# Batch 1's norms and turns moved one batch earlier, squares of batches 1 and 2 on GpSimd, dense work moved later

## The chip, the cores and the metric

One core of a Trainium2 chip. The metric is the time of one execution in microseconds (us), as the device measures it; several executions are taken of each kernel. PE is TensorE, PEld its weight loads, DVE VectorE, ACT ScalarE, POOL GpSimd. The span of a trace is 1.8 to 2.5 us shorter than the time of the same run. Each run is marked by its state; one run of experiment 5 and one of the kernel before beside it are marked slow and left out of the ratios, the single runs of experiments 13 to 15 are of unknown state, and all others are marked fast.

## The reference, cut to what matters

```python
q_n = q / (norm(q) + 1e-6);  k_n = k / (norm(k) + 1e-6)      # 8 batches, 12 heads, 448 x 64
attn = softmax(q_n @ k_n.T / tau)
x = (attn @ v), heads side by side                            # 3584 x 768
out = leaky_relu(x @ w_in) @ w_out                            # 768 -> 2048 -> 768
```

## The kernel before

Each batch has twelve visits (pair of heads p, half): scores of one half pair, then row sums and value products that are owed from an earlier group, then the norm work of the next batch, then dense work (the two-layer network on rows that are ready) until a budget is met, then turns. A turn is a transpose on TensorE of a pair's normalised q and k with copies by DVE. The dense work is a list that is worked off in order; the budget (in us, as the kernel's author estimated them) only sets how far each visit goes. Its first layer gives tiles, each followed by a Prelu (the leaky ReLU) on ACT; its second layer gives blocks of 16 matmuls.

```python
inp = ctx.enter_context(tc.tile_pool(name="inp", bufs=1))     # q_n and k_n: one buffer each
ppv = ... bufs=2   # row sums and value products (PSUM)
pmm = ... bufs=2   # dense tiles, second-layer blocks and turned pairs (PSUM)
...
def norm_squares(b, what, eng, ...):  eng.tensor_mul(sq, x, x)       # written into q_n / k_n
def norm_reduce(b, what, ...):        nc.vector.tensor_reduce(...)
def norm_root(b, what, ...):          nc.scalar Ln, then Exp(0.5 x)
def norm_inverse(b, what, ...):       nc.vector: + 1e-6, reciprocal
def norm_apply(b, what, eng, ...):    eng.tensor_tensor(x * 1/norm)  # 2 instructions a group
...
        if b == 1:                    # cut: visits 0 to 5 hold the norms of batch 1's groups 1 and 2
            elif n == 6:
                norm_sums(2, "q")     # squares and sums on DVE
            elif n == 7:
                norm_sums(2, "k")
            elif n == 8:
                norm_root(2, "q"); norm_inverse(2, "q"); norm_apply(2, "q", P)
            elif n == 9:
                norm_root(2, "k"); norm_inverse(2, "k")
                norm_apply(2, "k", V, 0, 1)
                norm_apply(2, "k", P, 1, 3)
    turns = {(0, 9): (1, 0), (0, 10): (1, 1), (1, 3): (1, 2), (1, 4): (1, 3), (1, 5): (1, 4, 5),
             (1, 10): (2, 0, 1), (1, 11): (2, 2, 3), (2, 1): (2, 4, 5)}
```

Two facts carry the argument. The squares are written into the tile that the normalised values will fill, and that tile has one buffer. And DVE, ACT and GpSimd each work off their own list in order, so an instruction waits for the one written before it even if it needs nothing from it: in the changed kernel's trace DVE starts to copy a pair at 101.47 us that TensorE had turned by 96.6, because six multiplies stand before it.

## Time and profile before

| | before |
|---|---|
| time | 478.54 us, median of 3 (477.88 to 478.78) |
| span of the traced run | 477.8 us (its time was 480.28 us; it is not among the three) |
| TensorE busy | 435.0 us, 91% |
| TensorE idle from 39.4 to 116.8 us | 13.6 us |
| of it behind DVE's reciprocals | 6.7 us |

TensorE is the bound and its idle time in batch 1's visits is the target. The prediction below shows the lines and how they are read.

### The profile page before, as it was taken

To read this page: it belongs to the slowest core of one execution; us is meant where nothing else is said; L and a number is where in the kernel's file an instruction comes from. 1 tells how busy PE (TensorE), PEld (TensorE's weight loads), DVE (VectorE), ACT (ScalarE), POOL (GpSimd) and SP (SyncE) were. 2 spreads that over 40 slices of the span, in tenths; PEclk is the share of its full clock that TensorE was granted. 3 is DMA by queue.
4 is the path that set the end of the run, shared out by engine and by line. 5 is a ranking of instruction groups with operands and counts; after the bars stand their busy time and mean duration, and the time that the engine had idled before them with its cause. 6 is when DMAs were issued, how large, how long until landed. Compare 5 with 4: busy or idle time off the path is not lost.

```text
span 477.8 us, 8541 instructions
## 1 busy us (share of the span) xinstructions
PE 435.0 (91%) x3632; PEld 221.9 (46%) x3632; DVE 219.4 (46%) x269; ACT 269.7 (56%) x445; POOL 126.6 (27%) x150
## 2 busy tenths in 40 slices
PE   0788976779899999989899999998999999999996
PEld 0465633444344554444344554444434554454463
DVE  5964677967913186206823186218711311321000
ACT  3765665736764557654674557664765567533411
POOL 6552308065083012800083013700180000000000
PEclk9999999979999999998999999999999999999999
DMA  9999991808629660393329560455034110020022
GB/s 118 211 200 203 187 168 34 115 1 122 85 45 135 137 109 2 66 213 56 56 48 135 133 108 1 59 125 92 0 59 92 58 42 1 18 66 18 0 67 66
DMA packets 73924, 41.23 MB, mean 86 GB/s; under 512 B 29600, under 2 KB 73120, under 8 KB 73888
## 3 DMA queue, kind: packets, MB, share of 16 engines
q0 software_dynamic: 37728, 22.81, 34.6%
q1 hardware_dynamic: 36160, 17.90, 16.2%
q8 instruction: 28, 0.46, 0.4%
q14 instruction: 8, 0.07, 0.0%
HBM read 45.61 MB, written 11.01 MB: 119 GB/s over the span
## 4 chain that ended last, share of the span: by engine, by line
PE 76%; DMA 9%; DVE 6%; issue 4%; ACT 3%; POOL 1%; SPq 0%; POOLq 0%; ACTq 0%
PE mm L319 29%; PE mm L306 28%; PE pv L239 11%; PE sc L206 7%; DMA w_in_sb<-in_moe_w_in_dram 5%; DVE rs L262 2%; DMA kT<-k_n 2%; ACT pe L234 2%; DMA qk_bf<-in_q_dram 2%; DVE k_ni L127 1%; DVE k_n L124 1%; DVE q_n L124 1%; ACT hT L311 1%; PE sc L224 1%; PE mm L180 1%
## 5 line engine op out<-in xcount | busy, mean ns | idle before, releaser
L234 ACT ACTIVATE pe<-sc 112x896 bf16<-112x896 f32 (+2 forms) x192 | 168.1, 917 | 15.3 <-PE sc L224 8.1
L306 PE MATMUL mm<-xT,w_in_sb 128*128 128x512 bf16 (+3 forms) x864 | 157.3, 335 | 1.3 <-ACT hT L311 0.9
L319 PE MATMUL mm<-w_out_sb,hT 128*128 128x384 bf16 x896 | 154.0, 327 | 0.0
L262 DVE RECIPROCAL rs<-pv 128x448 f32<-128x448 f32 (+2 forms) x27 | 71.4, 2644 | 157.2 <-PE pv L239 157.1
L319 PEld LDWEIGHTS <-hT 128*128 128x128 bf16 x896 | 84.9, 98 | 67.0 <-issue 13.6
L306 PEld LDWEIGHTS <-w_in_sb 128*128 128x128 bf16 x864 | 77.9, 99 | 76.6 <-issue 17.4
L311 ACT ACTIVATE hT<-mm 128x512 bf16<-128x512 f32 (+3 forms) x144 | 71.9, 502 | 69.4 <-PE mm L306 69.0
L325 ACT COPY osb<-mm 128x384 f32<-128x384 f32 x56 | 26.8, 478 | 104.6 <-PE mm L319 74.0
L152 POOL TENSOR_TENSOR q_n<-qk_bf,q_ni 112x512 bf16<-112x512 bf16 x40 | 41.3, 1061 | 103.5 <-DVE q_ni L145 64.4
L206 PE MATMUL sc<-qT,kT 64*128 64x448 bf16 (+1 forms) x336 | 50.2, 362 | 10.2 <-ACT pe L234 7.2
L239 PE MATMUL pv<-pe,v_bf 112*32 112x448 bf16 (+2 forms) x864 | 48.9, 349 | 9.6 <-DVE rs L262 9.5
L152 POOL TENSOR_TENSOR k_n<-qk_bf,k_ni 112x512 bf16<-112x512 bf16 x44 | 46.6, 1085 | 15.8 <-DVE k_ni L145 15.8
L239 PEld LDWEIGHTS <-v_bf 112*32 112x32 bf16 x864 | 21.6, 100 | 29.7 <-issue 19.1
L92 POOL DMA_DIRECT2D v_bf<-in_v_dram x8 | 7.6, 944 | 101.0 <-PE pv L239 101.0
L206 PEld LDWEIGHTS <-kT 64*128 64x128 bf16 (+1 forms) x336 | 13.2, 103 | 40.2 <-issue 36.0
L127 DVE TENSOR_REDUCE k_ni<-k_n 112x16 f32<-112x1024 bf16 (+1 forms) x12 | 27.4, 2284 | 0.3
L127 DVE TENSOR_REDUCE q_ni<-q_n 112x16 f32<-112x1024 bf16 (+1 forms) x12 | 27.4, 2284 | 0.3
L239 PE MATMUL pv<-pe,ones 112*32 112x448 bf16 (+2 forms) x432 | 24.8, 346 | 1.0 <-ACT pe L234 1.0
L281 DVE TENSOR_TENSOR xT<-pv,rs 128x384 bf16<-128x384 f32 (+2 forms) x30 | 14.3, 477 | 22.9 <-PE pv L239 21.4
L278 DVE TENSOR_TENSOR xT<-pv,rs 128x448 bf16<-128x448 f32 x24 | 15.0, 625 | 19.7 <-PE pv L239 18.4
L180 PE MATMUL mm<-ident,q_n 112*128 112x112 bf16 x72 | 7.8, 241 | 10.9 <-DVE q_n L152 10.7
L124 DVE TENSOR_TENSOR q_n<-qk_bf 112x1024 bf16<-112x1024 bf16 x21 | 14.1, 719 | 4.7 <-DMA qk_bf<-in_q_dram 4.7
(48 smaller groups left out, 154.9 us busy)
## 6 DMA issues: line engine op xcount, KB each, us to landing
v_bf<-in_v_dram POOLq DMA_DIRECT2D x8, 672.0 KB, 7.5
qk_bf<-in_q_dram POOLq DMA_DIRECT2D x6, 672.0 KB, 7.4
qk_bf<-in_k_dram POOLq DMA_DIRECT2D x6, 672.0 KB, 10.8
w_in_sb<-in_moe_w_in_dram POOLq DMA_DIRECT2D x4, 768.0 KB, 19.9
w_out_sb<-in_moe_w_out_dram POOLq DMA_DIRECT2D x2, 1536.0 KB, 27.5
out_dram<-osb SPq DMA_DIRECT2D x16, 168.0 KB, 2.4
out_dram<-osb SPq DMA_DIRECT2D x16, 144.0 KB, 2.1
out_dram<-osb SPq DMA_DIRECT2D x16, 120.0 KB, 2.0
```

Of the source, the lines that this page charges most:

```text
L124: eng.tensor_mul(sq, x, x)
L127: nc.vector.tensor_reduce(st[what + "i", b][:, g0:g1].rearrange("p g a t -> p (g a) t"), squares(b, what, g0, g1).rearrange("p g a t d -> ...
L152: eng.tensor_tensor(out=xn[:, g, j].rearrange("p t h d -> p h t d"), in0=x[:, g, 2 * j : 2 * j + 2], in1=ni_j.unsqueeze(3).to_broadcast([P ...
L206: nc.tensor.matmul(out=sc[:wide, a, :S], lhsT=kT[r, o : o + wide], rhs=qT[r, p * S : (p + 1) * S], start=True, stop=True,)
L234: nc.scalar.activation(out=pe, in_=sc, func=ACTF.Exp, scale=inv_tau)
L239: nc.tensor.matmul(out=dst[32 * a : 32 * a + 32, c0:c1], lhsT=weights(a, ki), rhs=st["pe", b, 2 * g + a // 2][:, ki, a % 2, c0:c1], start= ...
L262: nc.vector.reciprocal(st["rs", b, g][:, c0:c1], sm[:, c0:c1])
L278: nc.vector.tensor_mul(x[:, kt, 64:512], po, rs)
L306: nc.tensor.matmul(out=pm[:, :n], lhsT=w_in_sb[:, kt, m * 128 : (m + 1) * 128], rhs=st["x", b][:, kt, x0 : x0 + n], start=(kt == 0), stop= ...
L311: nc.scalar.activation(out=st["h", c][:, m, :n], in_=pm[:, :n], func=ACTF.Prelu, alpha=0.01)
L319: nc.tensor.matmul(out=po[:, :NH], lhsT=st["h", c][:, m, j0 : j0 + 128], rhs=w_out_sb[:, m, n * NH : (n + 1) * NH], start=(m == 0), stop=( ...
L325: nc.scalar.copy(out=osb, in_=po[:, :NH])
```

## The change

Its intent is to give TensorE less to wait for in batch 1's visits: batch 1's norms go where DVE and GpSimd were idle, DVE loses the squares, and some dense work goes from batch 0 into batch 1's visits to cover the waits there. Cut to its core:

```diff
+        if b == 0:
+            if n == 0:   both(1, 0, 1, "squares", P, P)
+            ...          # cut: sums, roots and multiplies of groups 0 and 1 up to visit 9
+            elif n == 11: both(1, 2, 3, "reduce")
+        elif n == 1:     both(1, 2, 3, "root"); load(2, "v")
+        elif n == 2:     both(1, 2, 3, "apply", V, P)
         elif n == 4:
+            step(2, "q", 0, 3, ("squares", P)); load(3, "q")
+        elif n == 5:
+            step(2, "k", 0, 3, ("squares", P)); load(3, "k")
         elif n == 6:
+            step(2, "q", 0, 3, ("reduce", V))
         elif n == 7:
+            step(2, "k", 0, 3, ("reduce", V)); step(2, "q", 0, 3, ("root", A))
+        elif n == 8:
+            step(2, "q", 0, 3, ("apply", P)); step(2, "k", 0, 3, ("root", A))
+        elif n == 9:
+            step(2, "k", 0, 3, ("apply", V))
-                norm_apply(2, "k", V, 0, 1)
-                norm_apply(2, "k", P, 1, 3)
     turns = {
-        (0, 9): (1, 0), (0, 10): (1, 1), (1, 3): (1, 2), (1, 4): (1, 3), (1, 5): (1, 4, 5), ...
+        (0, 7): (1, 0), (0, 8): (1, 1), (0, 10): (1, 2), (0, 11): (1, 3), (1, 3): (1, 4, 5), ...
     def budget(b, n):
-            return piece_end[1] * i / 27
+            return i if i <= 12 else 12 + (piece_end[1] - 12) * (i - 12) / 15
```

More of the change, by code (lines that the diff above doesn't have):

```diff
@@ L450, with step @@
         at[0] += 1
-    def second_part(n):
-        if n == 2:
-            norm_squares(1, "q", P, 0, 1)
-            norm_squares(1, "k", P, 0, 1)
-        elif n == 4:
-            norm_reduce(1, "q", 0, 1)
-            norm_reduce(1, "k", 0, 1)
+    def step(b, what, g0, g1, *steps):
+        for name, eng in steps:
+            if name == "squares":
+                norm_squares(b, what, eng, g0, g1)
+            elif name == "reduce":
+                norm_reduce(b, what, g0, g1)
+            elif name == "root":
+                norm_root(b, what, g0, g1)
+            else:
+                norm_inverse(b, what, g0, g1)
+                norm_apply(b, what, eng, g0, g1)
@@ new lines, in early, with both @@
+    def early(b, n):
+        def both(to, g0, g1, name, eq=None, ek=None):
+            step(to, "q", g0, g1, (name, eq))
+            step(to, "k", g0, g1, (name, ek))
+        if b == 0:
+            if n == 0:
+                both(1, 0, 1, "squares", P, P)
+            elif n == 2:
+                both(1, 0, 1, "reduce")
+            elif n == 3:
+                both(1, 1, 2, "squares", P, P)
+            elif n == 4:
+                both(1, 0, 1, "root")
+            elif n == 5:
+                both(1, 0, 1, "apply", V, P)
+            elif n == 6:
+                both(1, 1, 2, "reduce")
+            elif n == 8:
+                both(1, 1, 2, "root")
+                both(1, 2, 3, "squares", P, P)
+                load(2, "q")
+            elif n == 9:
+                both(1, 1, 2, "apply", V, P)
+                load(2, "k")
+            elif n == 11:
+                both(1, 2, 3, "reduce")
+        elif n == 1:
+            both(1, 2, 3, "root")
+            load(2, "v")
+        elif n == 2:
+            both(1, 2, 3, "apply", V, P)
+        elif n == 4:
+            step(2, "q", 0, 3, ("squares", P))
+            load(3, "q")
+        elif n == 5:
+            step(2, "k", 0, 3, ("squares", P))
+            load(3, "k")
@@ L460, in second_part @@
         elif n == 6:
-            norm_root(1, "q", 0, 1)
-            norm_root(1, "k", 0, 1)
+            step(2, "q", 0, 3, ("reduce", V))
         elif n == 7:
-            norm_inverse(1, "q", 0, 1)
-            norm_inverse(1, "k", 0, 1)
-            norm_apply(1, "q", V, 0, 1)
-            norm_apply(1, "k", P, 0, 1)
+            step(2, "k", 0, 3, ("reduce", V))
+            step(2, "q", 0, 3, ("root", A))
+        elif n == 8:
+            step(2, "q", 0, 3, ("apply", P))
+            step(2, "k", 0, 3, ("root", A))
+        elif n == 9:
+            step(2, "k", 0, 3, ("apply", V))
@@ L470, in after_scores @@
     def after_scores(b, n):
-        if b + 2 < B and b > 1 and n < 2:
+        if b < 2:
+            return early(b, n)
+        if b + 2 < B and n < 2:
             load(b + 2, "qk"[n])
@@ L474, in after_scores @@
             return
-        if b > 1 and n == 2:
+        if n == 2:
             load(b + 1, "v")
-        if b == 1:
-            if n == 0:
-                load(2, "q")
-                norm_sums(1, "q", 1, 2)
-                norm_sums(1, "k", 1, 2)
-            elif n == 1:
-                load(2, "k")
-                norm_root(1, "q", 1, 2)
-                norm_root(1, "k", 1, 2)
-                norm_sums(1, "q", 2, 3)
-                norm_sums(1, "k", 2, 3)
-            elif n == 2:
-                load(2, "v")
-                for what in "qk":
-                    norm_inverse(1, what, 1, 2)
-                    norm_apply(1, what, P, 1, 2)
-                norm_root(1, "q", 2, 3)
-                norm_root(1, "k", 2, 3)
-            elif n == 3:
-                for what in "qk":
-                    norm_inverse(1, what, 2, 3)
-                    norm_apply(1, what, P, 2, 3)
-            elif n == 5:
-                load(3, "q")
-            elif n == 6:
-                norm_sums(2, "q")
-                load(3, "k")
-            elif n == 7:
-                norm_sums(2, "k")
-            elif n == 8:
-                norm_root(2, "q")
-                norm_inverse(2, "q")
-                norm_apply(2, "q", P)
-            elif n == 9:
-                norm_root(2, "k")
-                norm_inverse(2, "k")
-                norm_apply(2, "k", V, 0, 1)
-                norm_apply(2, "k", P, 1, 3)
-        elif n == 2:
             norm_sums(b + 1, "q")
@@ L533 @@
     turns = {
-        (0, 9): (1, 0), (0, 10): (1, 1), (1, 3): (1, 2), (1, 4): (1, 3), (1, 5): (1, 4, 5), (1, 10): (2, 0, 1),
-        (1, 11): (2, 2, 3), (2, 1): (2, 4, 5),
+        (0, 7): (1, 0), (0, 8): (1, 1), (0, 10): (1, 2), (0, 11): (1, 3), (1, 3): (1, 4, 5),
+        (1, 10): (2, 0, 1), (1, 11): (2, 2, 3), (2, 1): (2, 4, 5),
     }
@@ L570 @@
                     exponential(1)
-                if b == 0:
-                    second_part(n)
-                else:
-                    after_scores(b, n)
+                after_scores(b, n)
                 fill(budget(b, n))
```

## The prediction

> **What bounds the kernel now.** I read the page first, then the waits of TensorE, then windows, then the chain of waits in the stretch that the change touches.
>
> ```profile
> span 477.8 us, 8541 instructions
> PE 435.0 (91%) x3632; PEld 221.9 (46%) x3632; DVE 219.4 (46%) x269; ACT 269.7 (56%) x445; POOL 126.6 (27%) x150
> PE   0788976779899999989899999998999999999996
> PEclk9999999979999999998999999999999999999999
> ```
>
> TensorE sets the time: it is busy 435 of 477.8 us, so everything a schedule can win lies in 43 us of idle time, and some of that (the first 10.66 us, the drain) is out of reach here. The row by slices (11.9 us each) shows where the rest lies: slices 6 to 9 (60 to 107 us), where batch 1 is attended to while the dense work of batch 0 runs. After about 136 us TensorE is close to full. One slice there has a lower granted clock.
>
> ```profile
> 39.40:61.80 22.40, 21.90 (x270) 15.16 (x269) 10.77 (x22) 14.07 (x30) 4.71 (x6) 1.00 1.36 192
> 61.80:85.00 23.20, 16.37 (x201) 9.04 (x200) 18.72 (x33) 13.93 (x25) 11.29 (x12) 1.00 0.60 94
> 85.00:116.80 31.80, 25.55 (x291) 15.75 (x290) 25.06 (x30) 18.38 (x37) 13.45 (x15) 0.89 0.47 67
> 98.00:100.00 2.00, 1.68 (x17) 0.56 (x17) 1.44 (x4) 0.00 (x0) 0.29 (x1) 0.50 0.03 8
> ```
>
> Columns: stretch, its length, busy time of PE, PEld, DVE, ACT, POOL, clock, DMA. Batch 0's second part (39.4 to 61.8) leaves TensorE 0.5 us idle; batch 1 (61.8 to 116.8) leaves 6.8 + 6.3 = 13.1 us, while DVE is at 80%. The last line shows the clock at half after the longest gap.
>
> ```profile
> PE pv L239 <- DVE rs L262: 7.7, 3, 5.4
> PE sc L206 <- ACT pe L234: 4.8, 6, 2.2
> PE mm L180 <- POOL k_n L152: 1.6, 1, 1.6
> PE sc L206 <- DVE kT L188: 0.8, 1, 0.8
> ...
> 85.02 1.81 DVE q_n L124 x3
> ...
> 90.13 1.90 DVE k_n L124 x3
> 92.05 3.35 DVE k_ni L127
> 95.40 2.88 DVE rs L262
> 98.32 1.68 PE pv L239 x12
> ```
>
> The waits (60 to 132 us), then the chain. TensorE stood 5.4 us at the second value product of batch 1's group 1: the two PSUM buffers of that kind were full, one held the row sums, and DVE took their reciprocal only after squares and sums of all of batch 2 (1.9+3.35+1.9+3.35 = 10.5 us in one piece). The ACT wait of 2.2 is the same kind: exponentials queued on ACT behind square roots that waited for DVE's sums.
>
> **What the Trainium skill says.** "TensorE: Matmul & The Clock Gate", section on the HAM clock gate: an idle window of about 3.4 us halves the clock, and it takes about as long to recover. The trace agrees: after 5.38 us idle the clock was 0.50 and 16 value products took 1.68 us instead of 0.94, 24 narrow matmuls 2.74 instead of 1.71, scores 0.91 instead of 0.58: 2.1 us lost. The same page (architectural detail) calls DVE, ACT and GpSimd strict FIFO; the two chains above are what that looks like. "SBUF — State Buffer", section "Who interferes with whom": a DVE instruction with two SBUF inputs and a GpSimd one that reads SBUF share a read port by an exclusive lock. The trace agrees: the DVE multiply of 112x512 took 0.63 and 1.53 us when GpSimd multiplied too, and GpSimd's took 1.29 and 1.49 instead of 1.04; DVE's starts at 51.0, GpSimd's at 51.2 and 52.5, about 1.45 us for one of each. The section also says a reduction never contends. "GPSIMD Engine Reference", engine selection, has two-input work about 2x slower there; here a square of 112x1024 took 1.905 us against 0.685 on DVE, 2.8x.
>
> **The change part by part.**
>
> 1. Norms and turns of batch 1 into batch 0. Gone from batch 1's visits on DVE: four squares (2.7), four sums (4.9); groups 0 and 1 finish in batch 0. This takes away the ACT wait of 2.17, the wait for GpSimd's k_n of 1.63 and for the copy of 0.78.
>
> 2. Dense work. The budget was 1.193 us a visit; now it is 1.0 in batch 0 and 1.348 after. Walking the list (0.67 a narrow tile, 2.65 a second-layer block), one block of 2.7 us moves from batch 0's end into batch 1, and the blocks fall into visits 1, 2 and 4. The one in visit 4 covers the reciprocal, so the wait of 1.29 at visit 5 goes.
>
> 3. Squares of batch 2 to GpSimd: 6 x 1.9 = 11.4 us there, 3.8 off DVE, between the sums. The wait of 5.38 and the clock's 2.1 change.
>
> Taken away at most: 2.17+1.63+0.78+1.29+5.38+2.1 = 13.4 us.
>
> Now what comes instead. I march the new order by hand with the trace's durations (scores 0.52, sums 0.77, values 0.87, tile of 128 columns 0.42, block 2.71, turned pair 0.41).
>
> (a) Group 2 of batch 1 lands late: issued at 29.8 and 33.6, and the trace gives 24.1 and 21.6 us to landing, so 53.9 and 55.2. GpSimd is in order: squares q to 55.8, k to 57.7, load of batch 2's q 1.0, and only then batch 1 group 1's k multiply: 59.75 and 60.75. TensorE is ready for pairs 2 and 3 at about 58.4 and 60.4: 1.4 + 0.3, say 1.5 us. Batch 1 starts at 61.2 (before: 61.8, but one block, 2.7 us, further and two turned pairs, 0.8, less).
>
> (b) DVE then has copies to 60.9, two sums to 63.3, copies to 64.0, and only then batch 0's last reciprocal (1.36) to 65.4. Visit 1's values want that buffer at 63.65: 1.7 us. New.
>
> (c) Batch 2's squares. The pool of q_n and k_n has one buffer, so they can't start before batch 1's last turn, visit 3, at about 73.1. GpSimd: q to 78.8, a load to 79.8, k to 85.5. DVE: sums of k to 88.85, only then the reciprocal of group 1, to 91.8. TensorE has its sums at 83.8, stands first at the dense tiles (their Prelu is on ACT behind k's root, which waits for the same sum) and then at the values: 85.5 to 89.7 and 91.0 to 91.7, 4.9 us. So the 5.38 does not vanish; it comes back 0.5 smaller, cut in two pieces.
>
> (d) All six multiplies of batch 2's k are now DVE's (before: two), while GpSimd does q's six. Alternating at 1.45 they last from 94.4 to about 102.3; without contention 6 x 0.65 = 3.9, to 98.3. The copies of turned pairs 0 and 1 stand behind them on DVE, and the next dense block needs a PSUM buffer of the same two. TensorE is there at 97.4: 1.6 to 5.6 us, middle 3.6.
>
> (e) Batch 2's visit 0 has no block any more, so visit 1's values see the whole reciprocal (2.96 less 0.87 and 0.52): 1.6 us.
>
> Sum of the new waits: 1.5+1.7+4.9+3.6+1.6 = 13.3, as much as was taken away. Two pieces exceed 3.4 us, so a clock dip of 2 us has about an even chance: +1. Against it, the same march laid over the kernel before falls 2.1 us short of its 77.3 us from 39.4 to 116.8; TensorE is that much later in fact, and waits set by DVE or GpSimd ((a) to (d)) shrink by it: -2. Some 0.5 us of small ACT waits (1.6 in all before) should go too. Net about -1.5 us. From batch 2's visit 2 on nothing differs, TensorE has no slack to lose it in and the gain or loss runs through to the end: 478.5 - 1.5 = 477.0 us.
>
> **The rivals.** First, the clean win: GpSimd really takes the squares aside, all 13.4 us go, only (e) is new: about 467 us. For it: slices 60 to 107 hold the idle time and DVE at 80% is the engine that caused it. Against it: the single q_n buffer and strict order, which leave GpSimd 11.4 us of squares between visit 3 and visit 7. Second, GpSimd or the port becomes the bound: (c) and (d) at full size, with two dips: some 482 us. For it: 1.45 us a pair, measured. Against: TensorE being later hides part. Third, the transfers: the squares of group 2 wait for data, and batch 2's q is issued at 57.7 instead of 54.0; with the 9.0 to 11.9 us to landing that its loads took before it is there by 69.6, and used from 73.1, so I expect nothing beyond (a).
>
> **Range and chances.** The terms (c), (d) and the clock are the loose ones, each by 2 to 3 us, in both directions: range 471 to 482. Faster than 2% needs 469.1 or less, a gain of 9.4 us: that is the first rival nearly whole, 0.09. Slower than 2% needs 488, which would take a second long wait that I don't see: 0.04. Within 2%: 0.87.
>
> **What would show it.** Right if the waits of TensorE between 55 and 120 us still sum to 10 to 15 us with other names: turns waiting for GpSimd's k_n near 59 us (a); values waiting for a reciprocal near 64 us (b); Prelu or reciprocal behind a k sum that itself waited for GpSimd's squares, near 85 to 91 us (c); a second-layer block waiting for a copy behind six k multiplies, near 97 us, each pair with GpSimd some 1.45 us (d). Batch 2 would then start its visit 2 within 3 us of 116.8. Wrong if TensorE is busy over 90% from 62 to 112, if the squares of batch 2 on GpSimd end before 83 us, or if the six multiplies take under 5 us; then the first rival holds. A low clock in slices where the kernel before had none would mean the second.

## The result, and the profile after

The changed kernel took 482.27 us (median of 4, 481.38 to 483.51) beside 478.21 us of the kernel before: ratio 1.0087, 95% interval 1.0059 to 1.0115. Taken again later with 22 runs it gave 481.65 us, ratio 1.0057 (1.0040 to 1.0075). A ratio is the mean time of one kernel's fast runs over that of the other's fast runs of the same rounds, so it is not quite the ratio of the medians. The change is a small loss where a small gain was forecast, and 482.27 lies just outside the range given.

The page of the changed kernel, its busy row for TensorE and the row of the granted clock in 40 slices:

```profile
span 479.3 us, 8521 instructions
PE 435.0 (91%) x3618; PEld 221.4 (46%) x3632; DVE 220.8 (46%) x267; ACT 269.3 (56%) x445; POOL 137.6 (29%) x152
PE   0788888758899999989899999998999999999996
PEclk9999999988999999998999999999999999999999
```

TensorE is busy the same 435 us (slow work counts as busy too). Of the hole in slices 6 to 9 the first two slices are filled, and a deeper one stands in slice 9 (96 to 108 us), with a low clock in two slices there instead of one.

The same three stretches as before (length, PE, PEld, DVE, ACT, POOL busy, clock, DMA):

```profile
39.40:61.80 22.40, 20.85 (x280) 14.54 (x280) 16.50 (x32) 14.98 (x34) 13.53 (x12) 1.00 1.20 170
61.80:85.00 23.20, 19.65 (x220) 10.80 (x213) 14.81 (x24) 15.91 (x27) 15.71 (x12) 1.00 0.88 134
85.00:116.80 31.80, 22.63 (x246) 12.87 (x246) 23.11 (x25) 14.47 (x30) 11.55 (x12) 0.89 0.57 76
```

Between 61.8 and 85 us TensorE gained 3.3 us of busy time, the intent of the change. Between 85 and 116.8 us it lost 2.9 again, and 1.1 before 61.8.

The waits of TensorE from 39 to 119.7 us (total, times, longest):

```profile
PE mm L319 <- DVE kT L188: 4.7, 1, 4.7
PE pv L239 <- DVE rs L262: 3.8, 3, 1.8
PE sc L206 <- ACT pe L234: 2.4, 5, 0.8
PE mm L306 <- ACT hT L311: 1.7, 3, 1.1
PE mm L180 <- POOL k_n L152: 1.5, 2, 0.8
...
```

The old longest wait, 5.4 us for a reciprocal, is gone. The new longest is 4.7 us, at a second-layer block that needs a PSUM buffer which DVE's copies of a turned pair have yet to free. Where it comes from, in the chain of waits (start, us, what):

```profile
72.87 5.44 POOL q_n L124 x3
78.31 0.92 POOL qk_bf L92
79.24 5.61 POOL k_n L124 x3
84.85 0.02 issue
84.87 3.35 DVE k_ni L127
88.22 2.88 DVE rs L262
...
94.16 7.38 DVE k_n L152 x6
101.54 0.30 DVE qT L188
101.84 0.31 DVE kT L188
102.15 0.05 issue
102.20 4.28 PE mm L319 x16
```

From 73 to 102 us almost every link is GpSimd's or DVE's: the squares on GpSimd, the sum that waits for them, the reciprocal behind the sum, the six multiplies of k, the copies behind those. The block at 102.20 takes 4.3 us, where the same block takes 2.77 at full clock. In this trace the half clock came a second time, after the next wait (16 value products took 1.67 us instead of 0.94):

```profile
102.20 4.27 PE L319 MATMUL mm<-w_out_sb,hT 128*128 128x384 bf16 x16 [4.66 <-DVE kT L188]
...
112.04 1.67 PE L239 MATMUL pv<-pe,v_bf 112*32 112x448 bf16 x16 [1.79 <-DVE rs L262]
113.64 3.68 PE L319 MATMUL mm<-w_out_sb,hT 128*128 128x384 bf16 x16
```

**One stretch, measured the same way in all traces.** Both kernels do the same work on TensorE between two instants: the first dense tile after the 0.5 us wait for ACT near 39 us, and the first tile of batch 1's 512-row piece (near 117 to 120 us). I took from TensorE's timeline the time between them, the sum of the waits of 0.15 us and more listed there, and the rest. A run of the first experiment below, whose clock was 1.00 throughout the stretch, has a rest of 62.7 us: that is the work at full clock, and what a rest has above it is slow work.

| trace | elapsed | waits | rest | of it slow | after the stretch |
|---|---|---|---|---|---|
| before, first | 77.85 | 13.24 | 64.61 | 1.9 | 360.5 |
| before, second | 77.66 | 11.57 | 66.09 | 3.4 | 358.9 |
| before, third | 78.81 | 11.34 | 67.47 | 4.8 | 358.8 |
| changed, first | 79.94 | 14.35 | 65.59 | 2.9 | 360.4 |
| changed, second | 80.07 | 14.90 | 65.17 | 2.5 | 358.6 |
| changed, third | 80.90 | 14.10 | 66.80 | 4.1 | 358.8 |

The mean grows from 78.1 to 80.3 us, 2.2 us. The waits grow by 2.4 (12.05 to 14.45), the rest does not (66.1 and 65.9). What follows the stretch varies by 1.7 us in both kernels alike. The changed kernel reaches the stretch 0.4 us sooner (38.9 against 39.3 us), so the spans of these traces differ by 1.7 us (478.5 against 476.8). So the loss lies in this stretch and is, on average, one of waits: the changed kernel's are 14.1 to 14.9 us, those of the kernel before 11.3 to 13.2, while the rests overlap.

### The profile page after: what moved, and what is told of

It is laid out like the page before. It is cut to its first block, busy times and chain, and to the rows that moved or that the text cites. A ratio compares the mean times of both kernels' runs of the same rounds, so it can differ in the third digit from the quotient of the medians.

```text
span 479.3 us, 8521 instructions
## 1 busy us (share of the span) xinstructions
PE 435.0 (91%) x3618; PEld 221.4 (46%) x3632; DVE 220.8 (46%) x267; ACT 269.3 (56%) x445; POOL 137.6 (29%) x152
## 4 chain that ended last, share of the span: by engine, by line
PE 76%; DVE 14%; DMA 3%; POOL 3%; ACT 2%; issue 1%; SPq 0%; POOLq 0%; ACTq 0%; DVEq 0%
PE mm L319 29%; PE mm L306 27%; PE pv L239 11%; PE sc L206 7%; DVE rs L262 3%; DVE k_ni L127 2%; DMA kT<-k_n 2%; DVE k_n L152 2%; DVE q_ni L127 2%; DVE q_n L152 2%; ACT pe L234 1%; POOL k_n L124 1%; POOL q_n L124 1%; PE sc L224 1%; PE mm L180 1%; DMA qk_bf<-in_q_dram 1%
## 5 line engine op out<-in xcount | busy, mean ns | idle before, releaser
L234 ACT ACTIVATE pe<-sc 112x896 bf16<-112x896 f32 (+2 forms) x192 | 167.9, 917 | 15.9 <-PE sc L224 10.2
L319 PE MATMUL mm<-w_out_sb,hT 128*128 128x384 bf16 x896 | 156.9, 332 | 4.7 <-DVE kT L188 4.7
L306 PE MATMUL mm<-xT,w_in_sb 128*128 128x512 bf16 (+3 forms) x850 | 155.1, 332 | 3.0 <-ACT hT L311 1.7
L306 PEld LDWEIGHTS <-w_in_sb 128*128 128x128 bf16 x864 | 76.5, 98 | 76.5 <-issue 18.1
L311 ACT ACTIVATE hT<-mm 128x512 bf16<-128x512 f32 (+3 forms) x144 | 71.8, 502 | 61.8 <-PE mm L306 61.2
L152 POOL TENSOR_TENSOR q_n<-qk_bf,q_ni 112x512 bf16<-112x512 bf16 x36 | 38.1, 1088 | 91.1 <-DVE q_ni L145 71.2
L152 POOL TENSOR_TENSOR k_n<-qk_bf,k_ni 112x512 bf16<-112x512 bf16 x40 | 41.8, 1071 | 7.8 <-DVE k_ni L145 4.7
L278 DVE TENSOR_TENSOR xT<-pv,rs 128x448 bf16<-128x448 f32 x24 | 14.9, 622 | 20.4 <-PE pv L239 19.2
L180 PE MATMUL mm<-ident,q_n 112*128 112x112 bf16 x72 | 7.7, 241 | 11.1 <-DVE q_n L152 10.5
L239 PEld LDWEIGHTS <-ones 112*32 112x32 bf16 x432 | 9.2, 97 | 13.1 <-issue 9.1
```

Source lines behind the costliest of these rows:

```text
L152: eng.tensor_tensor(out=xn[:, g, j].rearrange("p t h d -> p h t d"), in0=x[:, g, 2 * j : 2 * j + 2], in1=ni_j.unsqueeze(3).to_broadcast([P ...
L234: nc.scalar.activation(out=pe, in_=sc, func=ACTF.Exp, scale=inv_tau)
L239: nc.tensor.matmul(out=dst[32 * a : 32 * a + 32, c0:c1], lhsT=weights(a, ki), rhs=st["pe", b, 2 * g + a // 2][:, ki, a % 2, c0:c1], start= ...
L278: nc.vector.tensor_mul(x[:, kt, 64:512], po, rs)
L306: nc.tensor.matmul(out=pm[:, :n], lhsT=w_in_sb[:, kt, m * 128 : (m + 1) * 128], rhs=st["x", b][:, kt, x0 : x0 + n], start=(kt == 0), stop= ...
L311: nc.scalar.activation(out=st["h", c][:, m, :n], in_=pm[:, :n], func=ACTF.Prelu, alpha=0.01)
```

## The experiments

All ratios are to the kernel before on the same chip in the same rounds; the changed kernel itself is at 1.0057 by its longest series. A difference of two ratios is uncertain by about 0.3% where both kernels had 22 runs and by 0.3 to 0.5% where one or both had six, by the intervals given. "Slow work" and "half clock" are readings of the granted clock or of the same matmuls taking longer.

### 1. The k multiplies of batch 2 shared again

```diff
-            step(2, "k", 0, 3, ("apply", V))
+            norm_inverse(2, "k")
+            norm_apply(2, "k", V, 0, 1)
+            norm_apply(2, "k", P, 1, 3)
```

> The changed kernel with batch 2's k multiplies shared as in the kernel before: group 0 on DVE, groups 1 and 2 on GpSimd. My theory: the wait of TensorE at the second-layer block near 97 us (4.7 us, for a copy behind six k multiplies on DVE) falls under 2 us, and the half-clock stretch after it (block of 4.27 instead of 2.71 us) goes; part comes back as turns that wait for GpSimd's k: about 478.5 us, ratio to before 1.000. Rival, that the squares on GpSimd are what costs: no more than 1 us gained, about 481.5 us.

Measured: 475.54 us (6 runs), ratio 0.9928 (0.9899 to 0.9956). DVE, then TensorE at the place of the 4.7 us wait:

```profile
95.62 2.43 DVE L152 TENSOR_TENSOR k_n<-qk_bf,k_ni 112x512 bf16<-112x512 bf16 x2
98.09 0.39 DVE L188 COPY qT<-mm 128x448 bf16<-128x448 bf16 x1
```

```profile
98.42 0.58 PE L206 MATMUL sc<-qT,kT 64*112 64x448 bf16 x4
98.93 2.77 PE L319 MATMUL mm<-w_out_sb,hT 128*128 128x384 bf16 x16
103.02 0.37 PE L180 MATMUL mm<-ident,k_n 112*128 112x112 bf16 x4 [0.39 <-POOL k_n L152]
```

The copy comes 2.5 us after DVE's multiplies begin instead of 7.3, the block starts with no wait and at full clock, and only 0.39 us comes back as a wait for GpSimd. This one line of the diff, which the change's description in a few words does not even name, costs 1.3% (1.0057 against 0.9928), some 6 us. Over the stretch of the table this trace has 74.0 us, 11.3 of it waits and 62.7 of rest, against 80.3, 14.45 and 65.9 on average for the changed kernel: about half of the 6 us is waits (4.3 less at this place, some of it back at others) and half slow work. The trace is of a run 1.5 us under the median, with no slow work; the six runs' clocks lie between 0.986 and 1.000, so the share of slow work varies. Without this line the change is a gain. My estimate of 478.5 was too cautious; the rival is out.

### 2. The old budget

```diff
-            return i if i <= 12 else 12 + (piece_end[1] - 12) * (i - 12) / 15
+            return piece_end[1] * i / 27
```

> The changed kernel with the old budget of dense work alone. My theory: a second-layer block stands again before the turns of batch 2 and one in batch 2's first visit, so the 4.7 us wait falls by about 2.7 and the 1.8 us wait for a reciprocal in batch 2's visit 1 goes, while the 1.3 us wait in batch 1's visit 5 returns; fewer low-clock windows: about 478.5 us. Rival, that moving dense work into batch 1 is what the change lives from: slower than the changed kernel, 484 us or more.

Measured: 480.40 us (22 runs), ratio 1.0030 (1.0012 to 1.0048). The direction is right, the size is not: the wait behind the copy fell from 4.7 to 0.6 us and the reciprocal's wait in batch 2 went, as the theory says, and the wait in visit 5 came back (1.8 us). But a wait of 2.8 us came up at a dense tile whose Prelu stands on ACT behind k's root, and batch 1's turn near 59 us, which the moved block no longer precedes, waited 1.7 us for DVE and 1.8 for GpSimd.

### 3. Batch 2's squares back on DVE

```diff
-            step(2, "q", 0, 3, ("squares", P))          # visit 4; k in visit 5
-            step(2, "q", 0, 3, ("reduce", V))           # visit 6; k in visit 7
+            step(2, "q", 0, 3, ("squares", V), ("reduce", V))
```

> The changed kernel with batch 2's squares on DVE again, each just before its sum. My theory: GpSimd's squares with the wait for batch 1's last turn made the k sum end at 88.2 us; on DVE the four pieces would take 10.5 us from 80.3, to 90.8, so the wait before the second values grows by about 2.6 us: slower than the changed kernel, about 485 us. Rival, that the squares on GpSimd are the harm: faster than 480 us.

Measured: 483.96 us (6 runs), ratio 1.0100 (1.0068 to 1.0133). k's sum ended at 91.6 us instead of 88.2 (0.45 of it because the stretch began later), and the wait for the Prelu behind it grew from 1.1 to 3.7 us. So inside this change GpSimd's squares are worth some 0.4%, only just clear of the noise; they are not the harm. The rival is out.

### 4. Two buffers for q_n

```diff
+    inq = ctx.enter_context(tc.tile_pool(name="inq", bufs=2))
-            st[what + "n", b] = inp.tile(...)
+            st[what + "n", b] = (inq if what == "q" else inp).tile(...)
```

(k_n keeps one buffer; memory allows no more.)

> The changed kernel with two buffers for q_n (k_n keeps one, memory allows no more). GpSimd's squares of batch 2's q can start before batch 1's last turn, near 70.2 instead of 72.7 us, k's end near 82.4 instead of 84.8; the sum of k then waits for nothing on GpSimd and starts 1.2 us earlier, at 83.6. My theory: 1.2 us gained, about 481 us. Rival, that GpSimd's lateness sets all that follows: 2.4 us or more gained, under 480 us.

Measured: 480.33 us (22 runs), ratio 1.0021 (1.0001 to 1.0041), 0.36% under the changed kernel, 1.7 us. The trace shows the point: DVE's sum of k (86.86) follows that of q with no gap, where the changed kernel had 1.21 us of waiting for GpSimd, and the 4.7 us wait is untouched. That fits the 1.2 us of my theory; the gain of 1.7 us, uncertain by 1.3, lies between it and the 2.4 of the rival and can't tell them apart.

### 5. Only the norms of batch 1 moved

```diff
+    squares of batch 2 on DVE, its k multiplies shared, the old budget   (edits 1, 2 and 3 together)
```

> Of the change only the norms and turns of batch 1 moved into batch 0's second part: squares of batch 2 on DVE, its k multiply shared with GpSimd and the old budget, as before. My theory: three of the old waits go (2.2, 1.6, 0.8 us) and two new ones come (1.4 us each, at batch 0's last turns and at batch 1's visit 1), the 5.4 us behind batch 2's squares stays: 477 us, within 1 per cent of before. Rival, that moving the norms is what made the changed kernel slower: 481 us or more.

Measured: 479.11 us (22 runs, one of them slow), ratio 1.0016 (0.9995 to 1.0037). The move by itself is neither gain nor loss that these runs could show; I had expected a little gain. In its trace the old wait behind batch 2's squares is there as 3.9 us at a Prelu.

### 6. TensorE kept busy in the new wait

```diff
+                if b == 1 and n == 11:
+                    idle = ppv.tile([128, S], F32, name="pv")
+                    for _ in range(20):
+                        nc.tensor.matmul(out=idle, lhsT=w_in_sb[:, 0, 0:128], rhs=w_in_sb[:, 0, 0:S], ...)
                 fill(budget(b, n))
```

> The changed kernel with twenty matmuls of 448 columns, about 3.8 us, whose result nobody reads, in the 4.7 us in which TensorE waits for the copy behind the six k multiplies. They take no time from anything if the wait is real. My theory, that the low clock after the wait costs on top of it: the block after it takes 2.7 instead of 4.3 us, the clock over the run rises by 0.005 or so, and the kernel gains 1.5 to 3.5 us: 479 to 480.5 us. Rival, that the low clock costs nothing beyond the wait: 482.3 us unchanged.

Measured: 480.57 us (22 runs), ratio 1.0026 (1.0007 to 1.0046), 0.3% under the changed kernel although it does more work. TensorE's timeline (start, us, what, and in brackets the wait before it):

```profile
100.42 3.96 PE L583 MATMUL pv<-w_in_sb 128*128 128x448 bf16 x20
105.15 2.77 PE L319 MATMUL mm<-w_out_sb,hT 128*128 128x384 bf16 x16 [0.78 <-DVE kT L188]
...
113.49 1.01 PE L239 MATMUL pv<-pe,v_bf 112*32 112x448 bf16 x16 [1.79 <-DVE rs L262]
114.44 4.34 PE L319 MATMUL mm<-w_out_sb,hT 128*128 128x384 bf16 x16
```

The block behind the filled wait runs at full clock, 2.77 us instead of 4.27. The half clock then came one wait later, after only 1.79 us of idleness. The median clock over the runs rose from 0.987 to 0.993. So a long wait does cost something on top of itself, by the ratios about 1.5 us, at the low end of what I expected and uncertain by 1.2.

### 7 and 8. Putting edits together

Run 7 is edits 1 and 4 and this one, which puts batch 1's last sums behind batch 0's last reciprocal; run 8 is run 7 with the old budget.

```diff
-            elif n == 11:
-                both(1, 2, 3, "reduce")
-        elif n == 1:
+        elif n == 0:
+            both(1, 2, 3, "reduce")
+        elif n == 1:
```

> The changed kernel with three edits: k multiplies shared (as in the run that gave 475.5 us), two buffers for q_n, and batch 1's last sums put behind batch 0's last reciprocal instead of ahead of it. My theory adds up: 475.5 less 1.4 us (the wait for that reciprocal) less 1.2 us (k's sum earlier): about 473 us. Rival, that TensorE now meets these waits elsewhere: 475.5 us unchanged.

> The same three edits and the old budget. My theory: the 1.8 us wait for a reciprocal in batch 2's visit 1 goes, the 1.3 us in batch 1's visit 5 comes back, so within 1 us of the run without it, about 472.5 us. Rival, that the new budget is a gain of its own: 475 us or more.

Measured: run 7 474.31 us (6 runs), ratio 0.9903 (0.9864 to 0.9942); run 8 477.38 us (22 runs), ratio 0.9963 (0.9939 to 0.9987). Run 7's median is 1.2 us under run 1's, half of the 2.6 expected, and their intervals overlap widely, so that gain is not shown. Run 8 is a clear miss, and its rival holds: with the k multiplies shared, the new budget is worth 0.6%, while in experiment 2 it cost 0.3%, each not far above its noise. Its trace has the waits that the new budget covers: 1.9 and 1.8 us at batch 1's turn near 60 us, 1.8 at visit 5. A budget is good or bad only with what the other engines do meanwhile.

### 9. Only batch 2's squares on GpSimd, in the kernel before

```diff
+            elif n == 4: norm_squares(2, "q", P)         # k in visit 5
-                norm_sums(2, "q")
+                norm_reduce(2, "q")                      # visit 6; k in visit 7
```

> Of the change only the squares of batch 2 on GpSimd, in the kernel before; all else as before. There batch 1's last turn comes in visit 5, so with one q_n buffer GpSimd can't start them before about 84 us and ends near 95.5; k's sum ends near 99, a little later than the 95.4 of before. My theory: the 5.4 us wait grows by 2 to 4 us and the clock stays low after it: 480 to 483 us. Rival, that taking 3.8 us of squares off DVE helps by itself: 476 us or less.

Measured: 482.61 us (15 runs), ratio 1.0070 (1.0045 to 1.0094). GpSimd in its trace, and DVE's sum of k behind it:

```profile
86.79 5.60 POOL L124 TENSOR_TENSOR q_n<-qk_bf 112x1024 bf16<-112x1024 bf16 x3 [2.58 <-issue]
92.33 0.98 POOL L92 DMA_DIRECT2D qk_bf<-in_q_dram  x1
93.32 5.59 POOL L124 TENSOR_TENSOR k_n<-qk_bf 112x1024 bf16<-112x1024 bf16 x3
```

```profile
98.94 3.35 DVE L127 TENSOR_REDUCE k_ni<-k_n 112x48 f32<-112x3072 bf16 x1 [3.17 <-POOL k_n L124]
```

The squares wait for batch 1's last turn in visit 5, since q_n has one buffer, and TensorE's longest wait grows from 5.4 to 7.5 us. The trace is of the slowest of the 15 runs (487.0 us), and its times are some 3 us later than I expected. The same move that helps by some 0.4% inside the change hurts by 0.7% alone, as my theory said. That it is the turns in visit 3 that free the buffer in time rests on the traces (the first square starts at 72.7 us there and at 86.8 here) and on experiment 4; two q_n buffers in this kernel were not tried.

### 10 and 11. The version that beats both

Run 10 is run 7 with a budget 0.06 us higher after batch 0, which brings a second-layer block into batch 2's first visit, ahead of the value products that wait for a reciprocal. Run 11 is run 10 with batch 2's norms one or two visits earlier and, in batch 1's norms, both inverses ahead of the multiplies.

```diff
-            return i if i <= 12 else 12 + (piece_end[1] - 12) * (i - 12) / 15
+            return i if i <= 12 else 12.06 + (piece_end[1] - 12) * (i - 12) / 15
```

> The run of the three edits (k shared, two q_n, last sums later; 474.3 us) with the budget raised by 0.06 us after batch 0, which puts the last second-layer block of that stretch into batch 2's visit 0 instead of 1. My theory: the 1.8 us wait for the reciprocal in visit 1 goes, and with it the half-clock block that followed it: 471 to 472.5 us. Rival, that the low clock comes from the sparse stretch as a whole and the reciprocal's wait is hidden elsewhere: 474 us.

> That kernel with batch 2's norms two visits earlier, so that k's sum ends before group 1's row sums ask for their reciprocal, and with both inverses before the multiplies in batch 0. My theory: the 1.0 and 0.7 us waits near 89 us go, the turns' wait for GpSimd's k near 50 and 59 us falls by about 0.7 each: 469 to 470.5 us, 2 per cent under the kernel before. Rival, that two visits earlier GpSimd's squares collide with batch 1's own multiplies: 472 us or more.

Measured: run 10 472.22 us (6 runs), ratio 0.9848 (0.9811 to 0.9885); run 11 472.74 us (6 runs), ratio 0.9855 (0.9815 to 0.9895). Run 10 is as expected. The waits of TensorE left in run 10 up to 113 us:

```profile
PE mm L307 <- ACT hT L312: 2.5, 3, 1.8
PE sc L207 <- ACT pe L235: 2.4, 5, 0.8
PE mm L181 <- POOL k_n L153: 0.8, 2, 0.4
PE pv L240 <- DVE rs L263: 0.7, 1, 0.7
PE mm L181 <- ACT hT L312: 0.3, 1, 0.3
```

Its elapsed time over the stretch is 71.6 us, 6.2 of it waits, against some 78 and 12 of the kernel before. Run 11's trace is shorter still (70.2 us), but its times are not: exponentials now queue on ACT behind the earlier root, 1.7 us at the longest. That two runs' medians differ by 0.5 us says nothing at six runs each.

### 12. The changed kernel again

> The changed kernel itself again, for its clock in more runs and on the chip of the others. My theory: 481 to 483 us at a mean clock of 0.980 to 0.987, the kernel before 478 to 479 us at 0.985 to 0.989, and the time falls with the clock from run to run. Rival, that the first four runs of it fell badly: 479.5 us or less.

Measured: 481.65 us (22 runs), ratio 1.0057. The range was right. The clock explains nothing: its median over the runs is 0.987, at the upper edge of what I expected and the same as that of the kernel before. Within each kernel the time does fall with the clock from run to run, but the two kernels differ by 3 us at the same mean clock. That sent me back to the traces.

### 13 to 15. More traces of both

> The kernel before once more, for a second trace: the traced run of it was at a span of 477.8 us, while its other runs have a median of 476.2. My theory: the granted clock fell in other places, so that less work met it, or fewer times: span 475 to 476.5, the same waits of TensorE between 40 and 117 us to within 0.5 us, and the difference in slow matmuls. Rival: other waits, from the loads at the start.

> The same again, a third trace, for the spread: waits within 0.5 us of the other two, the slow work between 1 and 4 us.

> The changed kernel, a third trace: the waits of TensorE between 40 and 119 us within 0.7 us of the other two, and again 1 to 2 us above those of the kernel before; slow work 2 to 5 us.

Measured: 478.43, 479.14 and 480.48 us, one run each, so their state is not known; by their clocks (0.988, 0.984, 0.987) they are like the fast runs. They fill the table above. In the kernel before, the waits are not within 0.5 us of each other: the first trace has 1.7 and 1.9 us more than the others. In the changed kernel they lie within 0.8 us and, on average, 2.4 above, a little outside what I expected. From the second one:

```profile
71.04 0.40 PE L206 MATMUL sc<-qT,kT 64*112 64x448 bf16 x2 [0.41 <-ACT pe L234]
71.37 4.45 PE L319 MATMUL mm<-w_out_sb,hT 128*128 128x384 bf16 x16
77.14 0.59 PE L206 MATMUL sc<-qT,kT 64*112 64x448 bf16 x4 [0.78 <-DVE kT L188]
```

In the first trace that block took 2.77 us and a turn then waited 1.63 us for GpSimd's k. Here the block runs at half clock, takes 4.45 us, and there is no wait: elapsed 77.66 against 77.85. The third trace of the changed kernel shows the same exchange on the long wait:

```profile
66.26 4.46 PE L319 MATMUL mm<-w_out_sb,hT 128*128 128x384 bf16 x16
...
104.72 4.11 PE L319 MATMUL mm<-w_out_sb,hT 128*128 128x384 bf16 x16 [3.34 <-DVE kT L188]
```

TensorE is 1.7 us late from 66 us on and waits 3.34 instead of 4.66 us for the copy. A wait whose end another engine sets and slow work ahead of it are paid once, not twice. The last column of the table shows, too, that the first trace of the kernel before was of a slow specimen, though marked fast: 1.7 us more after the stretch than the other two.

### 16. The roots one visit later

```diff
-        elif n == 5:
-            step(2, "q", 0, 3, ("root", A))              # from run 11
         elif n == 6:
+            step(2, "q", 0, 3, ("root", A))
             step(2, "k", 0, 3, ("reduce", V))
```

(It also has the inverses of batch 1's norms as in the change, so two things differ from run 11.)

> The run with batch 2's norms two visits earlier, its q root one visit later and with batch 0's inverses as in the change, because the trace showed exponentials queued 1.7 and 0.5 us behind that root. My theory: those waits go: 470.5 us. Rival, that the low clock hides it: 472 us as the two runs before it.

Measured: 475.02 us (9 runs), ratio 0.9918 (0.9891 to 0.9945): a miss, slower than runs 10 and 11. The exponentials' waits went, but dense tiles now wait 2.05 and 1.29 us for a Prelu on ACT. Whether those two waits make up the whole difference I did not test. Run 10 stays the best.

## Why the prediction was right or wrong

The prediction said 477.0 us, a gain of 1.5; the kernel lost 2.7 us by its longest series and 4.1 by the medians of the first. Its mechanism was right: waits taken away are replaced by waits of about the same size with other names. What failed is the netting at the end of the sum.

Term by term, in the first trace of each kernel and by the mean of three traces of each:

| term | predicted | first traces | mean of three |
|---|---|---|---|
| taken away (waits of 2.17, 1.63, 0.78, 1.29, 5.38) | -11.3 | -11.3 | -10.2 |
| (a) turns wait for GpSimd's k near 59 us and, not predicted, at pair 0 | 1.5 | 0.85 + 0.68 | 2.1 |
| (b) values behind batch 1's last sums | 1.7 | 1.35 | 1.35 |
| (c) Prelu and reciprocal behind k's sum | 4.9 | 1.06 + 0.71 | 1.8 |
| (d) block behind the six multiplies | 3.6 | 4.66 | 4.2 |
| (e) reciprocal in batch 2's visit 1 | 1.6 | 1.79 | 1.8 |
| lateness of TensorE, taken off (a) to (d) | -2.0 | in the lines above | in the lines above |
| small waits, nearly all for ACT | -0.5 | +1.3 (1.99 before, 3.25 after) | +1.3 |
| slow work (2.1 taken away, 1 back) | -1.1 | +1.0 | -0.2 |
| sum | -1.6, given as "about -1.5" | +2.1 | +2.2 |

- **The list of waits, (a) to (e).** All five appeared at their places: 13.3 us predicted, 11.3 after the 2.0 taken off for TensorE's lateness, and 11.1 measured (11.25 by the mean). Experiments 1, 4 and 9 tie (d) and (c) to the causes named: the six multiplies on DVE, and the single q_n buffer with GpSimd's strict order. That the sum fits so well is partly luck, since (c) came 3 us smaller and (d) 1.1 larger: TensorE was 2.5 us late at (c), where it stood at 88.0 instead of 85.5 us, and not late at (d), where it stood at 97.5 instead of 97.4.
- **(d).** The prediction put it between 1.6 and 5.6 us and took the middle. The six multiplies took 7.38 us, close to its alternating case of 7.9 (six times its own 1.45 would be 8.7; where the rest goes it does not say), not to the 3.9 of no contention: GpSimd's own six began 1.6 us before DVE's and went on beside them nearly to the end. It is the largest of the new waits, and experiment 1 shows that it decides the sign: with those multiplies shared the kernel gains 0.7%.
- **The failing steps are three terms of the netting.** By the means the prediction missed by 3.8 us, and these make it up.
  - "Some 0.5 us of small ACT waits should go too": they grew by 1.3 us, a miss of 1.8. Of this, 0.84 and 0.32 us are at scores that wait for exponentials in visits 7 and 8, where dense tiles now stand among them on ACT; that is read from the order in the trace, and no experiment was made for it.
  - All 11.3 us of old waits counted as gained, read from one trace: the wait of 1.63 us for GpSimd's k is absent in the two later traces of the kernel before, where a slow block covers it. A miss of 1.1.
  - "Two pieces exceed 3.4 us, so a clock dip of 2 us has about an even chance: +1", with all of the old 2.1 us of slow work counted as gone, net -1.1: slow work grew by 1.0 in the first trace and is the same over three of each (66.1 and 65.9 us of rest), a miss of 0.9. Only (d), 4.66 us, was longer than 3.4 us, yet the half clock came twice in the first trace; it isn't tied to the one long wait, for when that was filled in experiment 6 it came after the next one, of 1.79 us.
- **The rivals.** The first, all 13.4 us gained, is refuted. The second, GpSimd or the shared port as the bound with two clock dips at some 482 us, has the right time and the two dips of the first trace, but not the right parts: it wants (c) and (d) at full size, and (c) came at 1.8 us of 4.9. In (d) DVE's list order and the slowing by GpSimd act together. DVE's multiplies took 1.2 us each in the changed kernel and in experiment 1 alike, so that run takes four of them away and not the slowing. Six at 0.65 us would have left a wait of about 1.2 us (an estimate from the trace: they would end at 98.1 and the copies at 98.7, with TensorE ready at 97.5); no run tests this. The chances were right in one respect: the result is within 2%. The third, transfers, showed nothing beyond (a).
- **What the prediction did not see.** It did not say what each part is worth alone. Tested apart, moving the norms is neutral, GpSimd's squares help inside the change (by little) and hurt without it, and one line on k's multiplies costs more than the whole loss.

Open remains why the spans of the three traces of each kernel differ by 1.7 us and the timed runs by 2.7 to 4.1; chance of the clock is likely and not shown. The runs scatter by 4 us within one kernel.

## What to carry to other kernels

When work moves to another engine, follow that engine's list in order to the next thing that the bound engine needs from it: six multiplies ahead of one 0.3 us copy cost more here than the whole change lost. A wait and slow work ahead of it are paid once, so compare the time elapsed between two fixed points of the same work in several traces, not sums of waits in one. A buffer count of one ties an early start on one engine to the last read on another; check it before moving work forward.

## What the Trainium skill lacked or had wrong

- "TensorE: Matmul & The Clock Gate", section on the HAM clock gate, asks for an idle window of about 3.4 us; a later section of the page says that frequent short idling can bring the low clock too, without a size. Here it followed a wait of 1.79 us in a sparse stretch (the next block took 4.34 us in experiment 6), one of 1.35 us (4.46 us in the third trace of the changed kernel) and, in the third trace of the kernel before, one of 0.47 us at 39.2 us (12 matmuls took 2.72 us instead of 1.47), after a wait of 1.42 us ahead of it; in experiment 1's trace no half clock appeared after waits of 1.79 and 1.35 us. The page's free-running window agrees with that scatter; what is lacking is how sparse a stretch is enough.
- No page has it that slow work ahead of a wait set by another engine costs nothing: blocks of 2.77 and 4.45 us led to the same elapsed time, 77.85 and 77.66 us, in two traces of the kernel before.
- "SBUF — State Buffer", section "Summary: rules for kernel authors", says that the second instruction blocks fully until the first has ended. DVE's six multiplies and GpSimd's six ran from 92.55 to 101.5 us, 9.0 us for both; one after the other, by their durations alone (0.65 and 1.04 us), they would take 10.1. So some of each instruction seems to overlap; GpSimd's spans in a profile are rough, and which part it is isn't shown.
- "GPSIMD Engine Reference", section on engine selection, gives about 2x for two-input work. Here a bf16 square of 112x1024 took 1.89 us on GpSimd against 0.68 on DVE, 2.8x, and a multiply of 112x512 by a broadcast 1.04 against 0.65, 1.6x.
